# Loading the q weights in two DMAs instead of one at the head of a layer's input queue

## The chip, the cores and the metric

The kernel runs on one core of a Trainium2 chip. The metric is the device time of one execution in microseconds. The time before is the median of three runs; beside it stands one profiled execution with its own time, from which all the rows below are taken.

## What is computed

The input is one sequence of 2048 tokens with 640 channels, in bf16. It is normalised once (a layer norm without weights), and two branches read the result: an attention in which every token looks at 8 earlier ones at a distance of 2, with 32 heads of 20 channels, and a dense MLP with 1536 hidden channels. The output is the input plus both branches.

```python
def _A_ref(x, wqkv, wo):
    H = 32; Dh = D // H
    W, dil = 8, 2
    qkv = (x @ wqkv).reshape(B, S, 3, H, Dh).transpose(2, 0, 3, 1, 4)
    q, k, v = qkv[0], qkv[1], qkv[2]
    idx = pos[:, None] - (jnp.arange(W) * dil)[None, :]      # masked where idx < 0
    ...
    attn = _softmax(logits, axis=-1)
    o = jnp.einsum("bhsw,bhswd->bhsd", attn, vg)
    return o.transpose(0, 2, 1, 3).reshape(B, S, D) @ wo

def _B_ref(x, w1, b1, w2, b2):
    h = _gelu(jnp.einsum("bsd,df->bsf", x, w1) + b1)
    return jnp.einsum("bsf,fd->bsd", h, w2) + b2

xn = _layernorm(x, axis=-1)
return x + _A_ref(xn, A_wqkv, A_wo) + _B_ref(xn, B_w1, B_b1, B_w2, B_b2)
```

## The kernel before

**Tiling.** The sequence is cut into 4 chunks of 512 tokens, and a chunk into 4 blocks of 128. A block is normalised with tokens on partitions, transposed to channels on partitions (five channel tiles of 128, KT = 5), and copied into `xnT`. The projections read `xnT` as the moving operand and a 128x128 piece of a weight tile as the stationary one. For every projection the kernel sums over the five channel tiles in PSUM.

**Weights.** `wqkv` holds three SBUF tiles of 128 partitions x 5 channel tiles x 640 columns (800 KB each), named `wq_sb`, `wk_sb` and `wv_sb` in the profile. Channel tile `ti` of a weight tile is what a matmul with channel tile `ti` of `xnT` needs. The two MLP matrices (both `w_sb` in the profile) are loaded in two halves each.

**The input queue.** Nearly all loads are issued by SP (SyncE), in the order in which they stand in the code: x block 0 (160 KB, line 136), the weights of q (line 142), of k (143), x blocks 2 and 3 (320 KB, 144), the weights of v (145), the four x blocks of the second chunk (640 KB, 146), and the two halves of the first MLP matrix (149). ScalarE issues the load of x block 1 and of the MLP bias at the same time. In the profile `load_x` is line 131 and `load_w` line 134.

**The start on the engines.** The order of all pieces of work is written out by hand in `ORDER` (line 42); every engine runs its share of it in that order, and waits where something isn't ready. Before the first projection TensorE runs matmuls on constants that nothing reads (line 449). The first chunk is taken block by block:

- `st00`, `rs00`, `rc00`, `xn00a`, `xn00b`: mean and variance of block 0 on VectorE (line 212, 214), the square root on ScalarE (248), the reciprocal (254), and the normalisation in two parts, channel tiles 0 and 1 and then 2 to 4 (268).
- `tp00a`, `tp00b`, `tc00a`, `tc00b`: transposes on TensorE (283), and their copies into `xnT` (288), the first on VectorE, the second on ScalarE.
- `ga`: the q projection of block 0 for channel tiles 0 and 1; `gb2`, `gb3`, `gb4`: the same for channel tiles 2, 3 and 4, one piece each. All are `q_piece` (352), which runs through the channel tiles in the outer loop and the five output tiles in the inner one.
- `gd`, `ge`: the q projection of block 1, for channel tiles 0 and 1 and then 2 to 4 (352).
- `gc0`, `gc1`, `gc4`: ScalarE moves q from PSUM to SBUF (374, 376).
- `hj...`: projections of two blocks at a time, k and v for blocks 0 and 1, then q, k and v for blocks 2 and 3 (383).

Blocks 2 and 3 follow: `st03a`, `st03`, `rs03`, `rc03`, `xn03`, `tp03`, then the same for block 2. Between the head of `ORDER` and `tp03` stands this stretch:

```python
... tc00a ga neg1 sq1 rs01 rc01 tc00b gb2 mean1 xn01
tp01 gb3 gb4 tc01a gd tc01b ho ge gc1 st03a st03 rs03 gc0 hj102 rc03 hc102 tb b1 hj101 hc101 st02a st02 rs02 hj100
hc100 xn03 tp03 tc03 pk hj202 rc02 xn02 tp02 tc02 ...
```

The lines that load, in full:

```python
load_x(0, 1)
nc.vector.memset(x_sb[:, 1, 0:16], 0.0)
nc.scalar.dma_start(x_sb[:, 1, :], x_nb[:, 1, :])
nc.scalar.dma_start(b1_rt[0:FT, :], B_b1.rearrange("(t p) -> t p", p=P))
```

Of the kernel before, what the change touches and what calls it, by code (L numbers as in the profile page):

```python
# [20 lines left out]
KT, FT = D // P, F // P  # L21
# [56 lines left out]
def kernel(  # L78
# [58 lines left out]
    nc.vector.memset(x_sb[:, 1, 0:16], 0.0)  # L137
    nc.scalar.dma_start(x_sb[:, 1, :], x_nb[:, 1, :])
    nc.scalar.dma_start(b1_rt[0:FT, :], B_b1.rearrange("(t p) -> t p", p=P))
    for a in range(1):  # L140
        ks = slice(a * KT // 1, (a + 1) * KT // 1)
        nc.sync.dma_start(wqkv[0][:, ks, :], wqkv_v[:, ks, 0:D])
    load_w(1)
    load_x(2, BPC)
# [652 lines left out]
```

## Time and profile before

| | |
|---|---|
| median of 3 runs | 205.88 us (205.72 to 205.92) |
| profiled execution, its own time | 206.31 us |
| its span | 204.5 us, 3231 instructions |
| TensorE (PE) busy | 200.3 us, 98% |
| VectorE (DVE) busy | 181.6 us, 89% |
| ScalarE (ACT) busy | 127.2 us, 62% |
| GpSimd (POOL) busy | 34.6 us, 17% |
| granted TensorE clock | 1.0 |
| DMA | 31.77 MB, mean 155 GB/s |
| weights of q: issue, time to landing | 1.21 us, 4.8 us |

The span is what the profiler sees between the first and the last instruction; the execution's own time has 1.8 us beside it. Matmuls are pipelined and their ends are modelled, so a busy TensorE isn't one at its peak. A row of the timeline gives the start, the time in us, the engine, the line, the operation with the tile that it writes and the one that it reads, and how many instructions are merged; in brackets stands how long the engine was idle before it and what released it. PEld is TensorE's weight load, SPq what SP issues. The share of busy time is a mean over stages with different limits, so a change at the start is read from the rows of the start.

### The profile page before, as it was taken

The numbers are of one execution on the slowest core, as the hardware profiler recorded it, in microseconds if no ns is written. First come the engines' busy times: TensorE is split into PE (matmuls) and PEld (weight loads), VectorE is DVE, ScalarE is ACT, GpSimd is POOL, SyncE is SP. The second block draws the span as 40 slices with busy tenths as digits, with TensorE's granted clock in tenths as the row PEclk, the third lists the DMA queues.
The fourth block names the chain that finished last, engine by engine and source line by source line (L and its number), as shares of the span: only waits on it lengthen the run. The fifth ranks groups of instructions, "written<-read, shape, count | busy, mean of one in ns | idle before, by whom it ended". The sixth has DMA issues, their size and how long they took to land.

```text
span 204.5 us, 3231 instructions
## 1 busy us (share of the span) xinstructions
PE 200.3 (98%) x1261; PEld 111.4 (54%) x1261; DVE 181.6 (89%) x226; ACT 127.2 (62%) x246; POOL 34.6 (17%) x49
## 2 busy tenths in 40 slices
PE   8999999999999999999999999999999999999994
PEld 3898565564464555554554554455554455555552
DVE  2699999499998997877999999999989999889991
ACT  5589999999957998846335825474525793111210
POOL 2000000430000243002260050003104224111120
PEclk9999999999999999999999999999999999999999
DMA  6999469899358399999999086005642997962153
GB/s 208 392 396 380 109 213 328 306 256 199 78 116 275 67 171 163 163 144 151 192 190 189 6 90 105 0 0 69 130 107 32 169 189 127 216 101 25 27 67 64
DMA packets 27335, 31.77 MB, mean 155 GB/s; under 512 B 9272, under 2 KB 22072, under 8 KB 27320
## 3 DMA queue, kind: packets, MB, share of 16 engines
q0 software_dynamic: 7408, 12.78, 39.0%
q1 hardware_dynamic: 19600, 18.58, 31.8%
q8 instruction: 10, 0.16, 0.4%
q10 hardware_dynamic: 312, 0.20, 0.3%
q14 instruction: 5, 0.04, 0.1%
HBM read 10.00 MB, written 7.54 MB: 86 GB/s over the span
## 4 chain that ended last, share of the span: by engine, by line
PE 75%; DVE 15%; DMA 5%; ACT 2%; issue 1%; SPq 1%; DVEq 0%; ACTq 0%
PE lo L631 23%; PE hps L595 20%; PE pps L339 17%; PE gps L383 7%; PE hi L633 6%; DVE half L436 5%; DVE half L471 5%; DMA x_sb<-e 3%; DVE half L563 3%; PE gps L352 1%; DVE half L582 1%; DMA x_sb<-in_A_x_dram 1%; PE L L479 1%; DVE oT L586 1%; PE tp L283 1%
## 5 line engine op out<-in xcount | busy, mean ns | idle before, releaser
L595 PE MATMUL hps<-xnT,w_sb 128*128 128x512 bf16 x240 | 55.6, 379 | 0.0
L436 DVE TENSOR_TENSOR half<-qT,kT 128x2560 bf16<-128x2560 bf16 x32 | 46.6, 1483 | 0.1
L631 PE MATMUL lo<-w_sb,hT 128*128 128x512 bf16 x144 | 41.3, 379 | 0.0
L595 PEld LDWEIGHTS <-w_sb 128*128 128x128 bf16 x240 | 23.1, 98 | 26.2
L471 DVE TENSOR_TENSOR half<-half 128x1024 bf16<-128x1024 bf16 (+1 forms) x44 | 36.5, 878 | 0.0
L638 ACT CAST osb<-lo 128x512 bf16<-128x512 f32 x15 | 8.8, 583 | 37.1 <-PE hi L633 18.3
L633 PE MATMUL hi<-w_sb,hT 128*128 128x128 bf16 x144 | 31.5, 219 | 0.0
L611 ACT ACTIVATE hT<-hps,b1T 128x512 bf16<-128x512 f32 x36 | 24.0, 692 | 6.5 <-PE hps L595 5.6
L563 DVE TENSOR_TENSOR half<-vT,x_sb 128x2560 bf16<-128x2560 bf16 x16 | 23.0, 1487 | 3.3 <-DMA x_sb<-e 3.3
L644 POOL DMA_DIRECT2D out_dram<-osb x15 | 13.7, 959 | 71.8 <-ACT osb L639 71.8
L573 POOL DMA_DIRECT2D half<-half x12 | 15.6, 1302 | 56.1 <-DVE half L563 56.1
L563 DVE TENSOR_TENSOR half<-vT,ax 128x2560 bf16<-128x2560 bf16 x16 | 23.0, 1481 | 1.8 <-PE L L479 1.8
L631 PEld LDWEIGHTS <-hT 128*128 128x128 bf16 x144 | 14.1, 98 | 17.2 <-issue 0.4
L631 PE MATMUL lo<-wo,oT 128*128 128x512 bf16 x80 | 23.1, 379 | 0.0
L339 PE MATMUL pps<-xnT,wq_sb 128*128 128x512 bf16 x75 | 18.5, 379 | 0.0
L339 PE MATMUL pps<-xnT,wv_sb 128*128 128x512 bf16 x75 | 18.3, 379 | 0.0
L339 PE MATMUL pps<-xnT,wk_sb 128*128 128x512 bf16 x75 | 18.0, 379 | 0.0
L633 PE MATMUL hi<-wo,oT 128*128 128x128 bf16 x80 | 16.9, 219 | 0.0
L176 ACT ACT_TABLE_LOAD x12 | 15.4, 1283 | 0.9 <-PEq L781 0.7
L633 PEld LDWEIGHTS <-hT 128*128 128x128 bf16 x144 | 14.1, 98 | 1.9
L582 DVE TENSOR_TENSOR half<-half 128x1280 bf16<-128x1280 bf16 x16 | 13.1, 820 | 0.8 <-DMA half<-half 0.8
L403 ACT CAST vT<-pps 128x512 bf16<-128x512 f32 x15 | 8.8, 587 | 6.9 <-PE pps L339 6.9
(91 smaller groups left out, 262.9 us busy)
## 6 DMA issues: line engine op xcount, KB each, us to landing
half<-half POOLq DMA_DIRECT2D x12, 640.0 KB, 6.9
w_sb<-in_B_w_dram SPq DMA_DIRECT2D x4, 960.0 KB, 11.6
out_dram<-osb POOLq DMA_DIRECT2D x15, 160.0 KB, 3.5
ax<-e SPq DMA_DIRECT2D x8, 256.0 KB, 4.1
x_sb<-e SPq DMA_DIRECT2D x8, 256.0 KB, 4.8
out_dram<-b2bc POOLq DMA_DIRECT2D x3, 640.0 KB, 9.7
x_sb<-in_A_x_dram SPq DMA_DIRECT2D x1, 1280.0 KB, 13.7
out_dram<-x_sb SPq DMA_DIRECT2D x2, 640.0 KB, 4.4
```

Of the source, the lines that this page charges most:

```text
L176: nc.scalar.activation(warm[:], nc.const_aps.tensor(0.0, [P, 1], F32), func)
L339: nc.tensor.matmul(ps[:], lhsT=wqkv_p[which][:, ti, to, :], rhs=xnT[:, ti, :], start=(ti == 0), stop=(ti == KT - 1),)
L383: nc.tensor.matmul(ps[:, to - a, :], lhsT=wqkv_p[which][:, ti, to, :], rhs=tiles["xnT", 0][:, ti, pair * 2 * P : (pair + 1) * 2 * P], star ...
L436: nc.vector.tensor_tensor(out=half[:, j, h], in0=q[:, :, at].unsqueeze(1).to_broadcast([P, W // 2, KT, P]), in1=window(k, h, at), op=ALU.mult,
L471: nc.vector.tensor_tensor(out=kept, in0=kept, in1=gone, op=ALU.add)
L563: nc.vector.tensor_tensor(out=half[:, j, h], in0=window(qkv_tile(n, 2), h, cs), in1=ax_view(n)[:, j, ws, :].unsqueeze(2).to_broadcast([P, ...
L573: nc.gpsimd.dma_start(a, b, accum_op=ALU.add, max_dma_last_dim=CUT)
L582: nc.vector.tensor_tensor(out=a, in0=a, in1=b, op=ALU.add)
L595: nc.tensor.matmul(ps[:], lhsT=w1_sb[:, ti, ft * P : (ft + 1) * P], rhs=tiles["xnT", n][:, ti, :], start=(ti == 0), stop=(ti == KT - 1),)
L611: nc.scalar.activation(hT, tiles["hps", n, ft][:], ACT.Gelu_apprx_tanh, bias=b1T[:, ft : ft + 1], scale=1.0)
L631: nc.tensor.matmul(lo[:], lhsT=lhs, rhs=rhs[:, 0:CH], start=first, stop=last)
L633: nc.tensor.matmul(hi[:, 0 : D - CH], lhsT=lhs, rhs=rhs[:, CH:D], start=first, stop=last)
```

## The change

The weights of q are loaded by two DMAs, channel tiles 0 to 2 (480 KB) and then 3 and 4 (320 KB), on the same queue and in the same place. The loop before ran once, over the whole tile. Everything behind these DMAs on the queue keeps its order, and `ORDER` is the same.

```diff
     nc.scalar.dma_start(b1_rt[0:FT, :], B_b1.rearrange("(t p) -> t p", p=P))
-    for a in range(1):
-        ks = slice(a * KT // 1, (a + 1) * KT // 1)
+    for ks in (slice(0, 3), slice(3, KT)):
         nc.sync.dma_start(wqkv[0][:, ks, :], wqkv_v[:, ks, 0:D])
     load_w(1)
     load_x(2, BPC)
```

## The prediction

> **What bounds the kernel now.** I read the shares of the chain that ended last, then its pieces in order of time from 0 to 14 us, then the timeline of that stretch, the landings of the DMAs, and the DMA rate by stretches. The chain's shares first:
>
> ```profile
> PE 75%; DVE 15%; DMA 5%; ACT 2%; issue 1%; SPq 1%; DVEq 0%; ACTq 0%
> ```
>
> TensorE carries three quarters of the chain. In order of time the chain runs through the load of the second x block (to 3.59), the statistics and the normalisation of the first block (to 5.38), the transposes, and from 6.09 the q projection; from there to 85 us it stays on PE without a break, and what follows starts from work that PE released. So a shift of PE's start is worth its full size at the end only if nothing else holds PE a few us later. Now what SP issues at the start:
>
> ```profile
> 0.74 0.41 SPq L131 DMA_DIRECT2D x_sb<-in_A_x_dram  x1
> ...
> 1.21 0.41 SPq L142 DMA_DIRECT2D wq_sb<-in_A_wqkv_dram  x1
> ...
> 1.68 0.52 SPq L134 DMA_DIRECT2D wk_sb<-in_A_wqkv_dram  x1
> ...
> 2.23 0.53 SPq L131 DMA_DIRECT2D x_sb<-in_A_x_dram  x1
> ...
> 2.80 0.48 SPq L134 DMA_DIRECT2D wv_sb<-in_A_wqkv_dram  x1
> ```
>
> and how long each takes from issue to landing (last number, us):
>
> ```profile
> wq_sb<-in_A_wqkv_dram SPq DMA_DIRECT2D x1, 800.0 KB, 4.8
> wk_sb<-in_A_wqkv_dram SPq DMA_DIRECT2D x1, 800.0 KB, 6.4
> wv_sb<-in_A_wqkv_dram SPq DMA_DIRECT2D x1, 800.0 KB, 8.2
> ...
> x_sb<-in_A_x_dram SPq DMA_DIRECT2D x1, 320.0 KB, 6.6
> x_sb<-in_A_x_dram SPq DMA_DIRECT2D x1, 160.0 KB, 2.5
> ```
>
> Issue plus duration gives the landings: q's weights at 1.21 + 4.8 = 6.0, k's at 8.1, x blocks 2 and 3 at 8.8, v's at 11.0. The issues are half a us apart, the landings 2.1, 0.7 and 2.2 us: the queue is fed far ahead of what it moves. What the compute engines make of these landings:
>
> ```profile
> 5.75 0.29 DVE L288 COPY xnT<-tp 128x256 bf16<-128x256 bf16 x1
> ...
> 6.05 0.89 PEld L352 LDWEIGHTS <-wq_sb 128*128 128x128 bf16 x15 [0.17 <-DMA wq_sb<-in_A_wqkv_dram]
> ...
> 6.09 1.00 PE L352 MATMUL gps<-xnT,wq_sb 128*128 128x128 bf16 x15
> ...
> 7.18 2.02 PEld L352 LDWEIGHTS <-wq_sb 128*128 128x128 bf16 x35
> ...
> 8.90 0.89 DVE L212 BATCH_NORM_STATS2 stats<-x_sb 128x6 f32<-128x320 bf16 x2 [0.97 <-DMA x_sb<-in_A_x_dram]
> 9.14 0.50 PEld L383 LDWEIGHTS <-wk_sb 128*128 128x128 bf16 x5
> ...
> 11.58 0.40 DVE L268 TENSOR_SCALAR xn<-x_sb,mv,rstd 128x640 bf16<-128x640 bf16 x1
> ...
> 12.05 0.37 PEld L283 LDWEIGHTS <-xn 128*128 128x128 bf16 x5
> ...
> 12.16 0.44 PE L283 MATMUL tp<-ident,xn 128*128 128x128 bf16 x5
> ```
>
> Two waits for a DMA matter. The first weight load of q waited 0.17 us for the DMA that the change splits. And VectorE waited 0.97 us for x blocks 2 and 3, which stand two places behind that DMA on the same queue; block 3's statistics, its normalisation (11.58) and its transposes (12.05) hang on that landing.
>
> **The change, part by part.** Against its own time (span 204.5, whole execution 206.31, so 1.8 outside the span) the sum is a difference; I carry that difference to the median of 205.88, 0.43 under the profiled execution.
>
> The first part (three channel tiles, 480 KB of the 800) stands where the whole stood. The remaining 320 KB (327,680 bytes) took 0.84 us at the 389 GB/s of these stretches, so the first part lands at about 5.2 and q's first weight load no longer waits: it could start at 6.05 - 0.17 = 5.88. But the matmul that uses it also reads the copy of the transposed block, which ended at 5.75 + 0.29 = 6.04. From the end of the first normalised part to the transpose that reads it, the chain shows 0.04 (5.38 to 5.42); the same step here gives 6.08 where the matmul started at 6.09. **Gain at the start: 0.01 us**, between 0 and the whole 0.17 if the copy were not in the way. I take 0.01, because the copy's row is there.
>
> The second part (320 KB) is read by the channel tiles 3 and 4, first in the group of 35 weight loads at 7.18. It lands where the whole landed, 6.0, plus what a second DMA costs: cover 1.1 us. It brings a wait of its own on PE. The first load of k's weights (9.14) carries such a satisfied wait and the 35 loads before it end at 9.20, with no idle noted; so 0, at most one slot of a weight load, 2.02 / 35 = 0.06. I take 0. Behind that wait on PE are the rest of the q pieces and, through their banks, ScalarE's evictions; they would be late only if the part landed after 7.18.
>
> One DMA more on SP takes one more issue: the next starts 0.47 us later (1.68 to 2.15), and so do all that follow on SP. The queue's backlog hides this: k's data are wanted by the engines at 6.0, their issue would end at 2.7; x blocks 2 and 3 at 8.1 against 3.2. Without that backlog x would land 0.47 late.
>
> What does a boundary between two DMAs cost on the queue? In the rate, with k landing at 8.1 and x at 8.8, there are two boundaries in one us:
>
> ```profile
> core 0: us, PE busy (x) PEld busy (x) DVE busy (x) ACT busy (x) POOL busy (x), PEclk, DMA share, GB/s
> ...
> 8.00:9.00 1.00, 1.00 (x22) 1.00 (x20) 0.10 (x1) 0.24 (x1) 0.00 (x0) 1.00 1.06 393
> 9.00:10.00 1.00, 1.00 (x14) 0.79 (x12) 0.96 (x3) 0.58 (x1) 0.00 (x0) 1.00 1.07 399
> ```
>
> 393 GB/s with them, 399 in the us after, which has none: 1.5% of 1 us, 0.015 for two. I take 0.01 to 0.02 for the added boundary, up to 0.1 by the rounding of the landings. So x blocks 2 and 3 land 0.02 later. What covers that: the normalised block 3 was ready at 11.58 + 0.40 = 11.98, its weight load could start at 12.02 and its matmul some 0.05 later (matmuls elsewhere follow their load by 0.04 to 0.06), but PE came to it at 12.16, being busy. Cover: 0.09 us. The same cover caps any gain: if PE came earlier than 12.07 it would wait for block 3.
>
> The Trainium skill speaks against this edit: DMA: Bandwidth & Descriptors, Rules for kernel authors, asks for 1 MiB or more in one DMA. Its fit for transfers issued from GpSimd (section Anatomy of one DMA), 2.0 us fixed and the bytes by 436 GB/s, makes 3.9 us of the whole and 3.1 + 2.8 of the parts, an estimate of 2.0 us more; by it the time would be about 207.8. This trace does not agree for DMAs queued back to back on SP, by the 393 and 399 GB/s above.
>
> Sum: -0.01 at the start, 0 for PE's wait, 0 for the issue, 0 for the boundary (0.02 under a cover of 0.09): **-0.01 us**, with ends at -0.09 (what the cover at 12.16 lets through) and +0.07 (0.1 of boundary less the cover, and one weight slot). That is no change: 205.9, and 205.75 to 206.0 with the spread of the runs (205.72 to 205.92). 0.2% of this time is 0.41 us, about what a measurement of this kernel can tell from no change.
>
> **The rivals.**
>
> *The second DMA isn't free on the queue* (slower). Place: x blocks 2 and 3, and so the transposes at 12.16. Price: the first x load, alone at the head of the queue, takes 2.5 us for 160 KB, of which 163,840 bytes at 392 GB/s are 0.42; 2.1 us are fixed. If each DMA paid that in turn, x would land 2.1 later, less 0.09 of cover: +2.0, 207.9. If only the issue's 0.47 came through: +0.38, 206.26. It decides from 0.09 on, and is over 0.2% from 0.50 on. Against it: landings 0.7 us apart for 320 KB, which leaves no room for 2.1, and the steady rate. For it: VectorE does wait for just this landing, there is next to no cover, and a bulk load that comes late anywhere in this queue (the x blocks of the next chunk too) has the same price. Chance 0.22, most of it at the small end.
>
> *The wait is larger than the profile shows* (faster). The 0.17 is from one execution, and its time is 0.43 from the median. The four loads of MLP weights on this queue, all of 960 KB, take from 11.1 to 12.4 us from issue to landing: 1.3 apart. If q's weights usually came half of that, 0.65, later against the x chain than here, the kernel before would start that much later and the first part, 0.84 earlier, would save some 0.5 to 0.6: 205.3. Against it: landings in the profile are at the pace of the rate, and the three timed runs lie within 0.2. Chance 0.15.
>
> *The readers wait for both parts*, if the dependence is kept for the whole tile: start at 6.0 + 0.02, time 205.9. Against it: the x tile is loaded in pieces too, and the statistics of block 0 start at 3.27 when only the first has landed. It gives the forecast's time.
>
> **How the numbers follow.** No change, by either way to it: 0.63. Slower by over 0.2%: 0.22. Faster by over 0.2%: 0.15. The likeliest is 205.9. The range reaches from 205.4, most of the faster case, to 206.5, which takes in the slower one where the issue's cost comes through (206.26) with the spread of the runs, and leaves out its large end.
>
> **What would show it.** In the profile of the changed kernel: two DMAs into q's tile, the first landing near 5.2 and the second near 6.0; no DMA noted at the weight load of q at about 5.9, its first matmul still at 6.08 or so; none at the group near 7.18; VectorE's wait for x ending at 8.90 to 8.95; the transposes at 12.16. The forecast is wrong if x blocks 2 and 3 land past 9.3, if PE idles at 7.18 or before 12.16, or if the first q matmul moves ahead by more than a tenth.

## The result, and the profile after

The kernel with the two DMAs is slower: 207.44 us in the median (206.89 to 208.79), beside 205.97 for the kernel before (205.72 to 206.17). The ratio is 1.0069, with a 95% interval of 1.0043 to 1.0094; of 205.97 us that is 1.4 us more (0.9 to 1.9). Here and below the ratio is an estimate over the runs, without three that took over 1% longer at a granted clock of 0.99, and need not be the quotient of the two medians. The profiled execution took 207.22 us with a span of 205.4, so against the profiled execution of before (206.31 and 204.5) it shows 0.9 us of it. The granted clock is 1.0 in both. The rows below are about that 0.9; for the other 0.5 of the median there is no trace.

First the landings of the DMAs of the first 5 us in the kernel after. The last number is the time from issue to landing.

```profile
wk_sb<-in_A_wqkv_dram SPq DMA_DIRECT2D x1, 800.0 KB, 7.0
wv_sb<-in_A_wqkv_dram SPq DMA_DIRECT2D x1, 800.0 KB, 8.8
...
wq_sb<-in_A_wqkv_dram SPq DMA_DIRECT2D x1, 480.0 KB, 4.0
wq_sb<-in_A_wqkv_dram SPq DMA_DIRECT2D x1, 320.0 KB, 4.8
x_sb<-in_A_x_dram SPq DMA_DIRECT2D x1, 320.0 KB, 7.3
```

With the issues at 1.21, 1.68, 2.20 and 2.71 (the next view), and v's at 3.29, q's first part lands at 5.2, its second at 6.5, k at 9.2, x blocks 2 and 3 at 10.0, v at 12.1. Before, q landed at 6.0, k at 8.1, x at 8.8 and v at 11.0. Everything behind the split is about 1.1 us later, although it was issued only 0.5 later.

Next the chain of waits of the kernel after, in order of time from 0 to 15 us (start, time, what):

```profile
1.21 0.41 SPq L141
...
1.68 0.48 SPq L141
...
2.20 0.47 SPq L134
...
2.71 7.33 DMA x_sb<-in_A_x_dram
...
10.06 0.90 DVE stats L211 x2
...
11.79 0.81 DVE stats L211 x2
...
12.82 0.32 DVE xn L267
...
13.19 0.45 PE tp L282 x5
```

Before, the early chain ran through the load of x block 1, ScalarE's sum over that block, and the square root and the normalisation of block 0 to the q projection. Now it runs along SP's issues, both of q's parts among them, into the load of x blocks 2 and 3, and from there by VectorE to block 3's transposes. The timeline of the same stretch:

```profile
0.78 5.07 PE L448 MATMUL idle<-const-bfloat16-1.0 128*128 128x512 bf16 x16 [0.78 <-PEq L780]
...
6.05 0.12 PEld L351 LDWEIGHTS <-wq_sb 128*128 128x128 bf16 x1
6.09 0.29 DVE L287 COPY xnT<-tp 128x256 bf16<-128x256 bf16 x1 [0.39 <-PE tp L282]
...
6.44 1.00 PE L351 MATMUL gps<-xnT,wq_sb 128*128 128x128 bf16 x15 [0.17 <-DVE xnT L287]
...
7.50 2.02 PEld L351 LDWEIGHTS <-wq_sb 128*128 128x128 bf16 x35
...
10.06 0.89 DVE L211 BATCH_NORM_STATS2 stats<-x_sb 128x6 f32<-128x320 bf16 x2 [1.83 <-DMA x_sb<-in_A_x_dram]
...
13.19 0.45 PE L282 MATMUL tp<-ident,xn 128*128 128x128 bf16 x5 [0.56 <-DVE xn L267]
```

No weight load of q names a DMA any more: the wait of 0.17 is gone. VectorE's wait for x ends at 10.06 and not at 8.90, 1.16 later. Block 3's transposes start at 13.19 and not at 12.16, 1.03 later, and PE stands idle for 0.56 in front of them. PE was also 0.35 later at the first q matmul (6.44 and 6.09), because the 16 matmuls on constants at the start took 5.07 us and not 4.23; that lies in front of the same wait and is taken up again below.

Last, the DMA rate by stretches of 1 us, the last column in GB/s. The kernel after:

```profile
core 0: us, PE busy (x) PEld busy (x) DVE busy (x) ACT busy (x) POOL busy (x), PEclk, DMA share, GB/s
...
4.00:5.00 1.00, 1.00 (x4) 0.29 (x3) 0.54 (x3) 0.87 (x5) 0.00 (x0) 1.00 1.00 334
5.00:6.00 1.00, 1.00 (x11) 1.00 (x10) 0.66 (x3) 0.97 (x3) 0.00 (x0) 1.00 1.03 311
6.00:7.00 1.00, 0.83 (x15) 0.73 (x13) 0.86 (x4) 0.68 (x2) 0.00 (x0) 1.00 0.95 344
7.00:8.00 1.00, 1.00 (x22) 1.00 (x20) 0.25 (x2) 0.00 (x0) 0.00 (x0) 1.00 1.03 371
8.00:9.00 1.00, 1.00 (x21) 1.00 (x20) 0.23 (x2) 0.48 (x1) 0.00 (x0) 1.00 1.03 378
```

and the kernel before, in the stretches that the prediction did not look at:

```profile
4.00:5.00 1.00, 1.00 (x9) 0.54 (x7) 0.53 (x3) 0.92 (x5) 0.00 (x0) 1.00 1.06 388
5.00:6.00 1.00, 0.58 (x6) 0.28 (x5) 0.89 (x3) 0.97 (x3) 0.00 (x0) 1.00 1.07 386
6.00:7.00 1.00, 0.96 (x18) 0.94 (x17) 0.70 (x4) 0.57 (x2) 0.00 (x0) 1.00 1.06 394
```

There is a hole in the rate. It shows from 4 to 5 us, where q's first part gives way to its second, and is deepest from 5 to 6, where q gives way to k. From 4 to 9 us the kernel after moves 54 + 75 + 50 + 21 + 15 = 215 KB less (388, 386, 394, 392 and 393 before), which at 390 GB/s are 0.55 us. That is half of the 1.16. The other half is that the loss is uneven. A load has landed when the last of its 16 landing events has come. In the trace the first of k's comes at 7.72 us and the last at 9.17, where before they came at 7.60 and 8.05: the quickest share of the load is 0.12 later and the slowest 1.12, and the engines wait for the slowest. For x blocks 2 and 3 the mean of the 16 events is 0.52 later, near the 0.55 of the missing bytes, and the last is 1.16 later.

### The profile page after: what moved, and what is told of

Read it like the earlier page. It is cut to its first block, busy times and chain, and to the rows that moved or that the text cites. A ratio compares the mean times of both kernels' runs of the same rounds, so it can differ in the third digit from the quotient of the medians.

```text
span 205.4 us, 3210 instructions
## 1 busy us (share of the span) xinstructions
PE 199.6 (97%) x1239; PEld 111.9 (54%) x1261; DVE 181.5 (88%) x226; ACT 127.4 (62%) x246; POOL 34.6 (17%) x49
## 4 chain that ended last, share of the span: by engine, by line
PE 91%; DMA 4%; DVE 1%; SPq 1%; issue 1%; ACT 0%
PE lo L630 27%; PE hps L594 25%; PE pps L338 24%; PE hi L632 8%; PE gps L382 5%; DMA x_sb<-in_A_x_dram 4%; PE L L478 1%; DVE stats L211 1%; SPq L141 0%; PE tp L282 0%; SPq L134 0%; DVE mv L213 0%; SPq L131 0%; DVE xn L267 0%; ACT std L247 0%
## 5 line engine op out<-in xcount | busy, mean ns | idle before, releaser
L630 PE MATMUL lo<-w_sb,hT 128*128 128x512 bf16 x137 | 40.1, 379 | 0.0
L630 PE MATMUL lo<-wo,oT 128*128 128x512 bf16 x75 | 22.3, 379 | 0.1
```

The source lines that it names most:

```text
L630: nc.tensor.matmul(lo[:], lhsT=lhs, rhs=rhs[:, 0:CH], start=first, stop=last)
```

## The experiments

The expectations name theories by letters. F: the engines that feed from the queue run dry at a seam in the data of q. P: the shape of the 3 + 2 load is what is slow. I: everything behind the split is issued later by one issue, and only that counts. L, a later form of I: the load right behind q must be issued some time ahead of the end of q's data. S: a DMA more in front of k is needed for the loss. All ratios are against runs of the kernel before on the same chip; the chip is not the same in all experiments.

### Split k in place of q (on the kernel before)

```diff
-    load_w(1)
+    for ks in (slice(0, 3), slice(3, KT)):
+        nc.sync.dma_start(wqkv[1][:, ks, :], wqkv_v[:, ks, D : 2 * D])
```

> q's weights in one DMA as before; k's weights, one place further back on the same queue, in two (three channel tiles, then two). Theory F (feed): at the head of the program the queue isn't yet fed ahead, so the DMA engines run dry at the seams of a split q; a whole q (2.1 us of data) lets the feed get ahead, so splitting k costs little: x blocks 2 and 3 land at 8.9 to 9.1 (8.88 before, 10.04 with q split), time within 0.3 us of before. Theory P (pattern): a transfer of three channel tiles and then two moves slower wherever it stands, by its shape: x blocks 2 and 3 again at about 10, +1.0 to +1.5 us.

Measured: 206.62 us beside 206.17, ratio 1.0019 (0.9998 to 1.0039), span 204.7. The timeline:

```profile
1.68 1.05 SPq L144 DMA_DIRECT2D wk_sb<-in_A_wqkv_dram  x2
...
8.92 0.89 DVE L213 BATCH_NORM_STATS2 stats<-x_sb 128x6 f32<-128x320 bf16 x2 [0.68 <-DMA x_sb<-in_A_x_dram]
```

The same two shapes one place further back leave VectorE's wait for x where it was, at 8.92, though x itself is issued at 2.77, 0.54 later than before. The rate from 4 to 7 us is 387, 387 and 393. So neither the shape nor one issue more for x is the cause of the late x; P falls. It matters which load is behind the seam.

### Hold k back by a write into its tile (first form, on the kernel before)

```diff
-    load_w(1)
-    load_x(2, BPC)
-    ...
     for w in range(1, W):
         nc.gpsimd.memset(mask[:, w, 0 : DIL * w], MASKED)
+    nc.gpsimd.memset(wqkv[1][:, 0, 0:256], 0.0)
+    load_w(1)
+    load_x(2, BPC)
+    ...
```

> q's weights in one DMA; the issue of k's weights, and of all that stands behind it on SP, is held back to about 2.2 us (1.68 before, 2.20 with q split) by a memset on GpSimd into k's tile that the DMA must wait for. No DMA is added. Theory I (issue): what hurts is that all later issues are 0.5 us late; then x blocks 2 and 3 land 0.5 to 1.2 us late and the time is +0.5 to +1.5. Theory F (feed, with a cost per DMA): the issue alone isn't what the queue waits for; x lands within 0.2 of before, time within 0.3.

Measured: 211.89 us, ratio 1.0279 (1.0251 to 1.0306), span 210.2. It missed its purpose. SP did not wait with k at the head: the loads behind k, which have nothing to wait for, went ahead of it, and k became the sixth load on the queue, where it had been the third, issued at 3.33. It landed at 12.9, and PE stood idle for 3.75 us in front of k's first matmul at 13.07. It only says what k costs in that place; the second form, below, does what this one was meant to do.

### Split q in five

```diff
-    for ks in (slice(0, 3), slice(3, KT)):
+    for ks in [slice(i, i + 1) for i in range(KT)]:
```

> q's weights in five DMAs of one channel tile each (160 KB, 0.42 us of data at 392 GB/s). Theory F: four seams added instead of one, each shorter than what the feed needs for a DMA: x blocks 2 and 3 land 2 to 4 us late (11 to 13 us), time +2 to +4. Theory I (later issue alone): four issues of 0.47, +1.9 on the issue, x at most 1.9 later than before. Theory P has no number for this shape; if shape alone mattered, one tile each is the shape of the x loads, which move at the full rate: about 0.

Measured: 208.74 us, ratio 1.012 (1.010 to 1.0139), span 206.2. k is issued at 3.56. The rate falls to 124 GB/s between 4 and 5 us:

```profile
4.00:5.00 1.00, 1.00 (x3) 0.29 (x2) 0.58 (x2) 0.98 (x4) 0.00 (x0) 1.00 0.73 124
```

x is there for VectorE at 10.96, PE waits 0.53 for k at 10.17, and block 3's transposes start at 14.08. x lands at 10.93, 0.9 later than with two parts and 2.05 later than before: just short of what F was to cost (11 to 13), and just over the 1.9 that the later issues alone were to cost at most. The time, 2.5 us more (2.1 to 2.9), lies within F's 2 to 4, so this kernel does not decide between the two. The hole is deep where five small loads stand in a row, but three seams more do not cost three times as much again.

### The kernel after, with the bias load on GpSimd

```diff
-    nc.scalar.dma_start(b1_rt[0:FT, :], B_b1.rearrange("(t p) -> t p", p=P))
+    nc.gpsimd.dma_start(b1_rt[0:FT, :], B_b1.rearrange("(t p) -> t p", p=P))
```

> The changed kernel, with the load of the MLP bias (3 KB) issued by GpSimd instead of ScalarE, so that one DMA fewer is issued by ScalarE and SP between 0.7 and 2.2 us. Theory F, with a feed that SP's and ScalarE's DMAs share: the loss shrinks by a third to a half, x blocks 2 and 3 at 9.3 to 9.7, time +0.3 to +1.0 instead of +1.5. If ScalarE's DMAs don't share the feed, or under theories I and P: as the changed kernel, x at about 10, +1.0 to +1.5.

Measured: 207.64 us, ratio 1.0072 (1.0053 to 1.0091), span 205.4; VectorE has x at 10.46, 0.4 later than in the kernel after, with the same span. No better than the kernel after: the small load that ScalarE issues at about the same time as q is not what disturbs.

### q whole, with the bias load put between q and k on SP (on the kernel before)

```diff
-    nc.scalar.dma_start(b1_rt[0:FT, :], B_b1.rearrange("(t p) -> t p", p=P))
     for a in range(1):
         ...
+    nc.sync.dma_start(b1_rt[0:FT, :], B_b1.rearrange("(t p) -> t p", p=P))
     load_w(1)
```

> q whole; the 3 KB load of the MLP bias moves from ScalarE to SP, between q's and k's weights. So k's weights and all behind them are issued about as late as with q split (2.2 instead of 1.7 us) and there is one seam more on SP's queue, but q's 800 KB stand in one piece ahead of it. Theory I (the later issue alone): x blocks 2 and 3 land at about 10, time +1.0 to +1.5 us. Theory F (the engines run dry when little data is queued ahead of a seam): 2.1 us of data ahead of it, so x at 8.8 to 9.1, time within 0.3 us of before.

Measured: 206.79 us beside 206.32, ratio 1.0037 (1.0008 to 1.0066), span 204.7. q is one DMA here, and only 3 KB stand between it and k. Still, the timeline has VectorE's wait 0.9 later than before, and the rate in the stretch from 5 to 6 us falls from 386 to 260:

```profile
2.25 0.40 SPq L134 DMA_DIRECT2D wk_sb<-in_A_wqkv_dram  x1
...
9.81 0.89 DVE L212 BATCH_NORM_STATS2 stats<-x_sb 128x6 f32<-128x320 bf16 x2 [1.83 <-DMA x_sb<-in_A_x_dram]
```

```profile
5.00:6.00 1.00, 1.00 (x12) 0.89 (x11) 0.80 (x3) 0.97 (x3) 0.00 (x0) 1.00 0.96 260
```

So 2.1 us of q's data queued ahead of k do not cover k's issue at 2.25. F, in the form in which an undivided q covers what follows, falls. What this kernel shares with the kernel after (k at 2.20) is the later k. The bias load is a DMA more in front of k, though, so S stood.

### The second part of q on ScalarE's queue

```diff
-    for ks in (slice(0, 3), slice(3, KT)):
-        nc.sync.dma_start(wqkv[0][:, ks, :], wqkv_v[:, ks, 0:D])
+    nc.sync.dma_start(wqkv[0][:, 0:3, :], wqkv_v[:, 0:3, 0:D])
+    nc.gpsimd.memset(wqkv[0][:, 3, 0:16], 0.0)
+    nc.scalar.dma_start(wqkv[0][:, 3:KT, :], wqkv_v[:, 3:KT, 0:D])
```

> q split three and two as in the changed kernel, but the second part is issued by ScalarE on its own queue, behind x block 1 and the bias, so SP's queue has as many DMAs as before and k is issued at 1.7. Theory F with a feed of its own for each queue, and theory I: the engines find work on either queue, x blocks 2 and 3 land at 8.8 to 9.2, time within 0.3 of before. Theory F with one feed for both queues (the descriptors are made one DMA after the other): as the changed kernel, x at 9.5 to 10, +0.7 to +1.5.

Measured: 208.62 us, ratio 1.0134 (1.0097 to 1.0171), span 206.4. The second part, issued at 2.00 on the other queue (behind GpSimd's write into its tile), needs 7.2 us and lands at 9.2. PE now waits for it:

```profile
9.23 2.15 PE L352 MATMUL gps<-xnT,wq_sb 128*128 128x128 bf16 x35 [1.51 <-DMA wq_sb<-in_A_wqkv_dram]
```

A second queue doesn't help: the part no longer stands ahead of k, it shares the time with it. The loss of 2.8 us (2.0 to 3.5) is more than either theory had. And though SP issues k at 1.68, as early as before, the rate from 4 to 8 us is only 319, 275, 337 and 294: k stands here right behind q's first part, 480 KB, and an issue at 1.68 isn't early enough for that, or the second queue disturbs; this kernel doesn't separate the two.

### Split q in four and one

```diff
-    for ks in (slice(0, 3), slice(3, KT)):
+    for ks in (slice(0, 4), slice(4, KT)):
```

> q split four channel tiles and one (640 KB, 160 KB). Theory F: the first seam has 1.7 us of data ahead of it instead of 1.3 and should do less harm, but the second part is only 0.4 us, so the seam to k comes at the same time as in the changed kernel; if the harm is made at the first seam, x at 9.0 to 9.5 and +0.2 to +0.7; if at k's, x at about 10 and +1.0 to +1.5. Theory I (k issued 0.5 later): the same as the changed kernel, +1.0 to +1.5.

Measured: 207.36 us, ratio 1.0053 (1.0035 to 1.0070), span 205.1. k is issued at 2.21, as with 3 + 2. The stretch from 4 to 5 us is whole now (387 GB/s, where 3 + 2 has 334), the one from 5 to 6 is not (325). VectorE has x at 9.71, the transposes start at 12.84. With the seam further back within q the first hole is gone, and x is 0.35 earlier; the hole behind q stays. The two ratios overlap, so a gain in time is not shown.

### The kernel after, with x blocks 2 and 3 ahead of k

```diff
-    load_w(1)
     load_x(2, BPC)
+    load_w(1)
```

> The changed kernel with x blocks 2 and 3 issued ahead of k's weights instead of behind them. The path of the harm, by the trace of the changed kernel: late x blocks, late statistics, late transposes of block 3 (PE idle before 13.19). If that is the path, x lands at 7 to 8, the idle time before those transposes goes, and a new wait stands at k's first weight load, which now lands behind x at about 9.5 to 10.2 where PE asks for it at 9.15 to 9.45: +0.3 to +1.0 instead of +1.5. If the harm is somewhere else (PE's start, a later stage), the time stays at +1.0 to +1.5 with no wait for k.

Measured: 207.29 us, ratio 1.0050 (1.0032 to 1.0069), span 205.0. x lands at 7.6 and VectorE no longer waits late for it, and the wait turns up at k:

```profile
2.19 0.47 SPq L131 DMA_DIRECT2D x_sb<-in_A_x_dram  x1
...
9.74 0.74 PE L382 MATMUL gps<-xnT,wk_sb 128*128 128x256 bf16 x5 [0.49 <-DMA wk_sb<-in_A_wqkv_dram]
```

It is not the x blocks as such that are slow, it is what comes through the queue behind q; whichever of the two stands last is waited for.

### q whole, k and all behind it issued later (on the kernel before)

To keep the order on SP, GpSimd writes a few columns into the tile of every later load, and more into k's. As in the first form, the loads behind q stand after the set-up of the constants in the code. Nothing is split, and no DMA is added.

```diff
+    nc.gpsimd.memset(wqkv[1][:, 0, 0:256], 0.0)
+    nc.gpsimd.memset(x_sb[:, 2, 0:8], 0.0)
+    nc.gpsimd.memset(wqkv[2][:, 0, 0:8], 0.0)
+    ...
     load_w(1)
     load_x(2, BPC)
     load_w(2)
```

> No DMA is split and none added. The issue of k's weights is held back to about 2.2 us (1.68 before, 2.20 with q split) by memsets on GpSimd into the tiles that k's and all later loads write; their order on SP stays. Theory L (lead): at this point of the program a load's data cannot move before 3.3 to 4.3 us after its issue, and q's data are through at 5.4; so the later issue alone makes the DMA engines run dry: x blocks 2 and 3 at 9.4 to 10.0, time +0.4 to +1.2 us, as with the bias on SP (9.79). Theory S (seam): the harm needs one more DMA on the queue; then x at 8.8 to 9.1 and the time within 0.3 us of before.

Measured: 207.51 us beside 205.97, ratio 1.0078 (1.0060 to 1.0096), span 205.8. The timeline:

```profile
2.13 0.37 SPq L134 DMA_DIRECT2D wk_sb<-in_A_wqkv_dram  x1
...
9.99 0.89 DVE L219 BATCH_NORM_STATS2 stats<-x_sb 128x6 f32<-128x320 bf16 x2 [1.76 <-DMA x_sb<-in_A_x_dram]
...
13.11 0.45 PE L290 MATMUL tp<-ident,xn 128*128 128x128 bf16 x5 [0.49 <-DVE xn L275]
```

This is the kernel after in every number that counts, 9.99 for 10.06, 13.11 for 13.19, an idle PE of 0.49 for 0.56, k's landing events spread over 1.47 us for 1.45, and a time 1.6 us above before (1.2 to 2.0), with one load of q. The rate from 5 to 9 us is 322, 329, 348 and 347. The time is above the 0.4 to 1.2 that L had forecast, the landing within its 9.4 to 10.0. **The later issue of k, and of what follows it, is enough for the whole loss.** S falls.

### The same with k held back longer, and shorter

Each of these three kernels has one of the added lines.

```diff
-    nc.gpsimd.memset(wqkv[1][:, 0, 0:256], 0.0)
+    nc.gpsimd.memset(wqkv[1][:, 0, 0:640], 0.0)    # k_later2
+    nc.gpsimd.memset(wqkv[1][:, 0:2, :], 0.0)      # k_latest
+    nc.gpsimd.memset(wqkv[1][:, 0, 0:8], 0.0)      # k_edge
```

> The same with a longer memset, k's weights issued at about 2.6. Theory L: 0.4 us more than with the issue at 2.2, x blocks 2 and 3 at 9.8 to 10.5, time +0.8 to +1.7. Theory S: as before, x at 8.8 to 9.2, within 0.3.

Measured: k issued at 2.46, 207.31 us, ratio 1.0062 (1.0049 to 1.0075), span 205.3; VectorE has x at 9.71. k is issued 0.33 us later than in the last kernel, and the loss is no larger, where L had x at 9.8 or later.

> As the kernel with k's weights issued at 2.13 (q whole, the issue of k and of all behind it held back by GpSimd memsets into their tiles), but with a memset of 8 columns instead of 256 for k: k issued at about 1.9. Theory L (the load right behind q must be issued some 3.3 to 3.7 us ahead of 5.4, when q's data are through): no or a small hole, x blocks 2 and 3 at 8.9 to 9.3, time within 0.4 us of before. It is the control too: if the memsets themselves, and not the time of the issue, made the loss, it stays at x 9.7 to 10.0 and +1.2 to +1.6.

Measured: k issued at 1.93, 206.50 us beside 206.16, ratio 1.0027 (1.0009 to 1.0044). VectorE has x at 9.30, the transposes start at 12.43, the rate from 5 to 6 us is 360.

```profile
1.93 0.37 SPq L134 DMA_DIRECT2D wk_sb<-in_A_wqkv_dram  x1
...
9.30 0.89 DVE L219 BATCH_NORM_STATS2 stats<-x_sb 128x6 f32<-128x320 bf16 x2 [1.33 <-DMA x_sb<-in_A_x_dram]
...
14.66 0.49 DVE L219 BATCH_NORM_STATS2 stats<-x_sb 128x6 f32<-128x320 bf16 x1 [1.59 <-DMA x_sb<-in_A_x_dram]
```

The writes by GpSimd are the same here as with k at 2.13, but for the size of the one into k's tile; so the writes as such don't make that kernel's loss, the 0.20 us between the two issues make most of it: 0.6 us here (0.2 to 0.9), 1.6 there. The profiled execution of this one has a span of 205.9, more than its first transposes explain. The last row shows where more was lost in it: VectorE waits 1.59 us for the x blocks of the second chunk, which take 11.0 us from their issue at 3.59, where before they took 9.3. The ratio is what I go by.

> The same with a memset of two channel tiles of k's weights, k issued at about 3.0. Theory L with a delay that each load needs from its issue: a lead of 2.4 us, so the hole grows by the 0.5 to 0.6 us that the issue is later than 2.46: x blocks 2 and 3 at 10.2 to 10.8, time +1.8 to +2.6 us. If the hole is of one size as soon as the load comes too late (as 2.13 and 2.46 were alike: x at 9.96 and 9.68): x at 9.6 to 10.1, +1.2 to +1.6.

Measured: k issued at 2.99, 206.79 us, ratio 1.0030 (1.0012 to 1.0048), span 205.1; VectorE has x at 9.67, the transposes start at 12.85. In this one q itself came late, at 6.74 (PE starts on it at 6.78), and still it lost less than with k at 2.13. L said that the loss grows with the delay: it does not. Nor does it stay of one size, as the other reading had it: 0.6 us (0.2 to 1.0) is clearly less than the 1.6 (1.2 to 2.0) with k at 2.13, though x lands only 0.32 earlier.

### Split q in one and four

```diff
-    for ks in (slice(0, 3), slice(3, KT)):
+    for ks in (slice(0, 1), slice(1, KT)):
```

> q split one channel tile and four. The first part's data are through at about 3.4, 1.7 us after the second part's issue at 1.68. Theory L with one fixed delay of 3.3 us or more: a hole of 1.5 us there, q's second part at 7.0 to 7.6, x blocks 2 and 3 at 10.2 to 10.8, +1.3 to +2.5. If a delay depends on how much was issued before (with q in five parts the second part's data did move at 3.6): no hole at 3.4, the hole at k's first data as in the changed kernel, x at 9.5 to 10, +0.7 to +1.5.

Measured: 208.93 us, ratio 1.0154 (1.0117 to 1.0192), span 207.0. The larger part is now the load right behind a short one, and it is the one that suffers, although it is issued at 1.67. It lands at 8.2, later than L had it (7.6 at most), the loss of 3.2 us (2.4 to 3.9) is larger too, and PE waits for it:

```profile
8.27 0.75 PE L351 MATMUL gps<-xnT,wq_sb 128*128 128x128 bf16 x10 [1.77 <-DMA wq_sb<-in_A_wqkv_dram]
```

### q whole, x blocks 2 and 3 ahead of k (on the kernel before)

```diff
-    load_w(1)
     load_x(2, BPC)
+    load_w(1)
```

> The kernel before with x blocks 2 and 3 issued ahead of k's weights. Theory L: x is issued at 1.68, as k was, and moves at 5.4; k is issued at 2.2 and wanted by the engines at 6.2, a lead of 4.0, enough or just not. x lands at 6.8 to 7.0, k at 8.9 to 9.3, where PE asks for it at 9.15. PE has nothing to gain before, since it doesn't wait there in the kernel before: within 0.3 us of before. If k comes at 9.3 or later, +0.2 to +0.5.

Measured: 206.04 us beside 205.97, ratio 1.0005 (0.9992 to 1.0018), span 204.3. x is issued at 1.68, right behind q, and k at 2.24; the rate stays at 392 and more from 4 to 9 us. So k may be issued at 2.24 without harm if another load stands between, issued at 1.68: what counts is the issue of the load right behind q. As a version it brings nothing.

### The kernel after, with x block 0 issued by ScalarE

SP then begins with q: both parts are issued at 0.74 to 1.73, and k at 1.78, nearly where it was before.

```diff
-    load_x(0, 1)
+    nc.scalar.dma_start(x_sb[:, 0, :], x_nb[:, 0, :])
```

> The changed kernel, with x block 0 issued by ScalarE ahead of x block 1, so that SP issues q's two parts at 0.74 and 1.21 and k at 1.68, as early as before the change. Theory L: k's lead is that of the kernel before or a little less, since q's data start a little earlier too; the hole at k's seam goes or shrinks, x blocks 2 and 3 at 8.7 to 9.4. x blocks 0 and 1 now share the DMA engines with q's first part and land 0.2 to 0.6 us later, PE starts by that much later: time +0.2 to +0.9. If the split itself makes the hole: x at about 10 and +1.3 to +2.0.

Measured: 208.93 us, ratio 1.0133 (1.0105 to 1.0161), span 205.8. That is 2.7 us more (2.2 to 3.3), where L had 0.2 to 0.9; a reason that the trace shows is named below. What this kernel is to show is the feed. The issues, and the rate from 4 to 7 us:

```profile
0.74 0.99 SPq L141 DMA_DIRECT2D wq_sb<-in_A_wqkv_dram  x2
...
1.78 0.46 SPq L134 DMA_DIRECT2D wk_sb<-in_A_wqkv_dram  x1
...
2.29 0.53 SPq L131 DMA_DIRECT2D x_sb<-in_A_x_dram  x1
...
6.86 0.63 PE L282 MATMUL tp<-ident,xn 128*128 128x128 bf16 x5 [1.01 <-DVE xn L267]
```

```profile
4.00:5.00 1.00, 1.00 (x4) 0.29 (x2) 0.84 (x3) 0.00 (x0) 0.00 (x0) 1.00 1.05 384
5.00:6.00 1.00, 0.84 (x7) 0.57 (x5) 0.00 (x0) 0.79 (x3) 0.00 (x0) 1.00 1.07 392
6.00:7.00 1.00, 0.14 (x2) 0.11 (x2) 0.71 (x3) 0.97 (x4) 0.00 (x0) 1.00 1.06 396
```

q is split and there is no hole; x blocks 2 and 3, issued at 2.29, take 6.7 us and land at 9.0, where the kernel after has 10.0. k's landing events lie within 0.45 us, as before. The split itself does no harm to the feed once its second part and k are issued early. But x blocks 0 and 1 now both come by ScalarE's queue and land at 3.7 and 5.2, where before they landed at 3.2 and 3.6, and PE stands idle for 1.01 us before the first transposes at 6.86: the place on the queue that this kernel gives to q it takes from x. The profiled execution is the fastest of the six, with a span 1.3 above before; the rest of the 2.7 is not explained by it.

### The runs side by side

These are the kernels in which the whole of q stands on SP's queue ahead of k, in one part or two. Issue of k (or, with an asterisk, of the load right behind q), and the landing of x blocks 2 and 3:

| kernel | load behind q issued | x blocks 2, 3 there | ratio |
|---|---|---|---|
| before | 1.68 | 8.88 | 1 |
| x first, q whole | 1.68* | 6.85 | 1.0005 |
| q split, x block 0 by ScalarE | 1.78 | 8.97 | (x blocks 0, 1 late) |
| k held back least | 1.93 | 9.28 | 1.0027 |
| k held back | 2.13 | 9.96 | 1.0078 |
| after | 2.20 | 10.04 | 1.0069 |
| q in 4 + 1 | 2.21 | 9.69 | 1.0053 |
| bias on SP | 2.25 | 9.79 | 1.0037 |
| k held back longer | 2.46 | 9.68 | 1.0062 |
| k held back longest | 2.99 | 9.64 | 1.0030 |

Up to 1.78 the landing loses nothing, between 1.78 and 2.13 it slips by 1.0 for 0.35 in the issue, and beyond that it stays between 9.6 and 10.0. The ratio follows it only roughly: with x between 9.64 and 9.79 it lies anywhere from 1.0030 to 1.0062.

## Why the prediction was wrong

The forecast was no change, 205.9 with a range to 206.5; the time, 207.44, is above it. By its own steps:

**The first part.** It was to land at about 5.2 and does. The wait of 0.17 at q's first weight load was to go and goes. That it would bring 0.01 and no more, because the copy of the transposed block ends just as late, can be read in the 4 + 1 run, whose matmuls on constants took 4.64 us: its first q matmul is at 6.09, as before, with q's first part there at 5.5. In the kernel after that start is at 6.44, not 6.08, but by the longer matmuls on constants; the run with k split has the same 6.44 with one DMA for q.

**The second part.** No DMA is noted at the group of 35 weight loads (7.50). The added wait on PE costs nothing, as said, but with less cover: the part landed at 6.5, not 6.0.

**The issue on SP.** This is the step that failed: "One DMA more on SP takes one more issue: the next starts 0.47 us later", and then "The queue's backlog hides this", priced at 0. The size of the issue was nearly right: k's issue moved by 0.52, from 1.68 to 2.20. But the backlog was argued from when SP's issue would end, 2.7, and when k's data were wanted, 6.0, a margin of 3 us, and no run shows that such a margin is enough; held back by 0.45 with q whole and no DMA added, k makes the full loss. So the issue of the load right behind q was no term of 0. Its delay, priced "without that backlog" at 0.47, came out as 1.16 at the landing of x and 1.03 at the transposes.

**The boundary.** The 0.01 to 0.02 was read from the stretch of 8 to 10 us of the kernel before, 393 and 399 GB/s, where loads issued 6 us earlier follow each other. That row is right for its place, as the run with k split shows by its 393 and 394 GB/s from 6 to 8 us, around the seam within k. It does not speak for 4 to 6 us, near the head of the queue; I took a rate from where the queue was long ahead for the place where it was not yet.

**The cover.** 0.09 at block 3's transposes was nearly right: of x's 1.16, 1.03 arrive there, so it was 0.13. The sum had the matmul start 0.05 behind its weight load; in the kernel after, both start at 13.19.

**The end.** In the kernel after the shift at the transposes arrives at nearly its full size, as said for a PE that nothing else holds a few us later: 1.03 there, 0.9 in the span. This is one execution of each. In others the two differ more: 0.78 at the transposes and 0.2 in the span with the bias on SP, 1.43 and 0.9 with the bias on GpSimd, 0.27 and 1.4 with k held back least. That a shift of PE's first matmul alone is not worth it shows in the runs with x first or k split: q's first matmul at 6.44, block 3's transposes at 12.47, and spans of 204.3 and 204.7 beside 204.5.

**The rivals.** The one that came true is "The second DMA isn't free on the queue". Its place (x blocks 2 and 3, VectorE, the transposes at 12.16) was right, and it had a chance of 0.22. Its price lay between its two ends, 0.38 and 2.0: neither the issue's 0.47 nor a fixed cost of 2.1 for each DMA, but 1.03 at the transposes. I set the range by its small end. The landings 0.7 apart that were held against it were those of loads far behind the head. "The readers wait for both parts" is refuted: q's first weight load at 6.05 is ahead of the second part's landing at 6.5. "The wait is larger than the profile shows" gave nothing that can be seen.

The Trainium skill's fixed 2.0 us for each DMA (DMA: Bandwidth & Descriptors, Anatomy of one DMA), which the prediction set against the rate, is a figure for transfers issued from GpSimd; by it the time would have been about 207.8, and it came out at 207.4. The runs do not bear out the reason: the split of k, a DMA more on the same queue, cost 0.4 us (0 to 0.8) with no loss of rate, and holding k back, with no DMA more, cost 1.6.

**What is shown and what is open.** Shown: a later issue of the load right behind q makes the hole and the loss without a split, and a split with early issues makes no hole. Open: why a load has to be issued before about 1.8 us to follow without a hole on data that end near 5.3 (an estimate: x blocks 0 and 1 and q are 1.147 MB, and the rates of before, 19, 296, 312, 388 and 386 GB/s from 1 us on, have moved that much by then). It is no fixed lead from each load's issue, or the loss would grow from 2.13 to 2.99. It is not the time of the issue alone either: behind a shorter load, in one and four, an issue at 1.67 was too late. That the hole does not close again, with the rate below 380 up to 9 us, is seen in the kernel after and in most of the kernels with k after 2.1; the spread of k's landing events (0.45 us without a hole, 1.45 and 1.47 with one) shows that some shares of a load lose over 1 us and others hardly any, but these views do not show what the DMA engine of a late share does in that time.

## What to carry to other kernels

A DMA more on an issuing queue is priced by what it does to the issue time of the load right behind it, and near the start of a program that load may be more sensitive than the times from issue to landing suggest: look at the DMA rate in the very stretch where the one load gives way to the next, not in a later one. A wait of 0.17 us at the head is worth little when the second load behind it has a consumer with 0.09 us of cover; find that consumer before touching the queue. Where a seam is wanted, try it at a load further back, as with k here, and hold the next load back without a split before blaming the split.

## What the runs showed of the hardware

- The landing of x behind k reacts to the issue of k in a step: 8.97 with k issued at 1.78, 9.28 at 1.93, 9.96 at 2.13, and 9.6 to 10.0 beyond, though by the estimate above data of the load before k were still moving until about 5.3.
- The Trainium skill (DMA: Bandwidth & Descriptors, Latency and other measured facts) gives about 600 ns to the first byte for DMAs issued from engines like SP. If k needed no more than that, a k issued at 2.13 would have been ready to move by about 3.1 (its issue ends at 2.50), an estimate, and there would be no hole; the 322 GB/s from 5 to 6 us, against 386 before, do not agree.
- The same page (Issuing engines are not separate DMA queues) says that issuing from several engines saves only sequencer time, usually small beside the DMA itself. That the queues share the same engines agrees with the second part of q on ScalarE's queue, 7.2 us from issue to landing; the issue time is small here too, 0.41 us for q beside 4.8 to the landing, but its effect is not: 0.45 us of later issue cost 1.6 (1.2 to 2.0).
- The hole is uneven over the 16 landing events of a load: the first of k's is 0.12 us later than before, the last 1.12. A mean rate 14 and 19% down in two stretches of 1 us (388 to 334, 386 to 311) hides that.
- The same 16 matmuls on constants take 4.23 us in the profiled execution of before, 4.64 with 4 + 1 and 5.07 in the kernel after; with q whole 4.23 and 5.06 are both found. PE's first q matmul is at 6.09 with 4.23 and at 6.44 with 5.06 and 5.07. Each kernel has one profiled execution, so whether this goes with the kernel or changes from one execution to the next is not shown.
